# Two attention and two FFN layers on one core: a start with products on zeros, split weight loads, a shifted norm and a last tile in halves

## The chip, the core and the metric

The kernel runs on one core of a Trainium2 chip. Its engines run side by side and wait for one another through semaphores: TensorE (PE in the profile, with PEld for its weight loads), VectorE (DVE), ScalarE (ACT), GpSimd (POOL) and SyncE (SP), which issues all DMAs here. Every engine works through its own instructions in the order in which the program writes them. The metric is the device time of one execution in microseconds, the median of several.

## What is computed

Four layers on x of 2048 rows by 1024 columns: linear attention (A), a gated FFN (B), then A and B again with the same weights. Each normalises its input first and adds its result to x.

```python
def _A_ref(x, wqkv, wo):                      # H = 32 heads of 32
    q, k, v = heads(x @ wqkv)
    pq, pk = phi(q), phi(k)                   # t+1 where t > 0, exp(t) elsewhere, + 1e-6
    kv = einsum("bhsd,bhse->bhde", pk, v);  z = einsum("bhsd->bhd", pk)
    o = einsum("bhqd,bhde->bhqe", pq, kv) / (einsum("bhqd,bhd->bhq", pq, z)[..., None] + 1e-6)
    return merge(o) @ wo
def _B_ref(x, w_gate, w_up, w_down):          # 1024 -> 3584 -> 1024
    return ((x @ w_gate) * (x @ w_up)) @ w_down
for f in (A, B, A, B): x = x + f(layernorm(x))
```

## The kernel before

x stays on chip as 16 tiles `X[:, t, :]` of 128 rows. The order is written by hand (`manual_schedule`): what a function emits first runs first on its engine. Pools of buffers (`slots` of 128x4096 bf16, `temps` of 128x512 float32, `banks`, the 8 PSUM banks) are queues from which `get` takes the oldest.

**The start.** SP issues the loads in the order x0, x1, k0, x2, x3, k1, x4, v0, x5, x6, v1, x7 to x15 (lines 90 to 113): an x tile is 256 KB, k0, k1, v0, v1 are weight slabs of 1 MB (`load_cols`: 8 rows of 512 columns for each of 128 partitions). Then the preamble (the last loop of the kernel) runs, for the tiles t = 0 to 3, `ln_stats` (two `bn_stats` and a `bn_aggr` on DVE) and `ln_norm` (a Ln and an Exp on ACT, then the normalising `tensor_scalar` on DVE, L170); for tile 0 also `tr_tile`: eight transposes on PE (L187) into a PSUM bank and one copy on ACT (L188) into the transposed buffer xnT.

**Layer A, first stage** (`layer_A`, `kv_chunk`). 64 steps; step 0 is tile 0 with k0, step 1 tile 0 with k1, step 2 tile 1 with k0, step 3 tile 1 with k1, and so on: eight products (L369) each, then `phi` (an Exp on ACT, L193; two operations on DVE, L194 and L195) or, for v, a copy. The transposes of tiles 1, 2 and 3 are hung on steps 0, 1 and 3. So PE runs: step 0, transposes of tile 1, step 1, transposes of tile 2, steps 2 and 3, transposes of tile 3, step 4. ACT runs: Ln and Exp of tiles 0 to 3, the Exp of step 0, the copy of tile 1, the Exp of step 1, the copy of tile 2. All later tiles are transposed by DMA.

**Layer A, second stage.** Steps i = 0 to 43. A step emits `den_step(i-4)` (one product L501, Ln and Exp on ACT, a multiply on DVE, L509), `q_step(i)` (eight products L487 and `phi`) and `out_step(i-12)` (eight products L517, then the addition to X on DVE, L519). Eight L509 (c = 0 to 7) make the left operand of eight `out_step`s; the first of these is one step behind the last L509. In the first layer A steps 12 to 17 also carry maxima over the down weights on DVE (L222). `ahead_of` hangs the preparation of the FFN on these steps: for the tiles u = 0 to 7 `ln_stats` at 18+2u, `ln_norm` at 19+2u, the DMA transpose at 20+2u; loads of FFN weights (22, 28), their casts on ACT (25 to 28, 34 to 37), their sums on DVE (35, 41: L327), the sums of the transposed input (`t_sums`, 36 to 39: L349 to L357), and two loads and a POOL cast of down weights (36, 38, 40).

**Layer B.** `quad` (products L646) for the gate and up weights, then `down_seven` (products L868) for the down weights, in two passes over halves of the rows. In the last of seven stretches of the last pass (`final and i == 4`) the four tiles run one after the other: 14 products, an addition on DVE (L841) and a store of 128 KB (L768) for each.

Of the kernel before, what the change touches and what calls it, by code (L numbers as in the profile page):

```python
# [34 lines left out]
def kernel(  # L35
# [49 lines left out]
    def v3(s, n):  # L85
        return s[:].rearrange("p (k n) -> p k n", n=n)
# [4 lines left out]
    def load_x(t):  # L91
        nc.sync.dma_start(out=X[:, t, :], in_=x_view[:, t, :])

    def load_cols(view, n):
        s = slots.get()
        nc.sync.dma_start(out=v3(s, NB), in_=view[:, :, n * NB:(n + 1) * NB])
        return s

    nc.scalar.preload_act_table_set("natural_log_exp_and_others")
    wA = {}  # L100
    load_x(0)
    load_x(1)
    wA["k"] = [load_cols(wqkv_v, DC)]
    load_x(2)
    load_x(3)
    wA["k"].append(load_cols(wqkv_v, DC + 1))
    load_x(4)
    wA["v"] = [load_cols(wqkv_v, 2 * DC)]
    load_x(5)
# [2 lines left out]
    for t in range(7, NT):  # L112
        load_x(t)

    ident = const.tile([P, P], BF16, tag="ident", name="ident")
    make_identity(nc, ident[:])
    mask = const.tile([P, P], F32, tag="mask", name="mask")
# [33 lines left out]
    xqs = {}  # L151
    lns = {}

    def ln_stats(li, t):
        mv = small.tile([P, 2], F32, tag="mv", name="mv")
        st = small.tile([P, NST, 6], F32, tag="st", name="st")
        for c in range(NST):
            nc.vector.bn_stats(out=st[:, c, :], in_=X[:, t, c * FMAX:(c + 1) * FMAX])  # L158
        nc.vector.bn_aggr(out=mv[:], in_=st[:])
        lns[(li, t)] = mv  # L160

    def ln_norm(li, t):
        mv = lns[(li, t)]
# [10 lines left out]
    def tr_tile(li, t):  # L174
        xn = lns.pop((li, t))
        g, tl = divmod(t, TPG)
        if (li, g) not in xnTs:
            xnTs[(li, g)] = slots.get()
        s = xnTs[(li, g)]
        xnT = (h3 if li % 2 == 1 else v3)(s, NB)  # L180
        if (li, g) != (0, 0):
            nc.sync.dma_start_transpose(out=xnT[:, :, tl * P:(tl + 1) * P], in_=xn[:])
            return
        b = banks.get()
        pt = b[:].bitcast(BF16).rearrange("p (k n) -> p k n", n=P)
        for k in range(KD):
            nc.tensor.transpose(out=pt[:, k, :], in_=xn[:, k * P:(k + 1) * P], identity=ident[:])  # L187
        nc.scalar.copy(out=xnT[:, :, tl * P:(tl + 1) * P], in_=pt)  # L188
        banks.put(b)

    def phi(b, dst):
# [583 lines left out]
    def down_seven(q, li, p, hs, wd, load_piece, cast_piece, ORDER, at, run, finish, xrow, nl, W2, load_a, final):  # L775
        sg = [slots.get(), slots.get()]

        def blocks(r):
            v = hs[r][:].bitcast(F16).rearrange("p (u a g t) -> p u a g t", a=2, g=2, t=G)
            return [v[:, :, a, g, :] for g in range(2) for a in range(2)]  # L780

        def sview(r):
            return h3(sg[r // 4], G)[:, 2 * (r % 4):2 * (r % 4) + 2, :]

        def s_sum(i, r):
            a11, a12, a21, a22 = blocks(r)
            o = sview(r)
            x, y, op = {5: (a21, a22, ALU.add), 6: (o, a11, ALU.subtract), 3: (a12, o, ALU.subtract),
                        7: (a11, a21, ALU.subtract)}[i]
            nc.vector.tensor_tensor(out=o, in0=x, in1=y, op=op)  # L790

        def lhs(i, j, tl):
            if i in (1, 2, 4):
                v = blocks(j // 2)[{1: 0, 2: 1, 4: 3}[i]][:, j % 2, :]
            else:
                v = sview(j // 2)[:, j % 2, :]
            return v[:, tl * P:(tl + 1) * P]

        cast_piece(1)
        for i in range(2, 2 * len(ORDER)):  # L800
            at((i - 1) * WPC, cast_piece, i)
        for pi, i in enumerate(ORDER[:-1]):
            nx = ORDER[pi + 1]
            if nx in (5, 6, 3, 7):
                for r in range(NQD // 2):
                    at(pi * NQD + 2 * r + 1, s_sum, nx, r)
        if nl[0] < 4:
            for u in range(2 * TPG if p == 0 else TPG):
                t = nl[1] * 2 * TPG + u
                at(2 + 7 * u, ln_stats, nl[0], t)  # L810
                at(4 + 7 * u, ln_norm, nl[0], t)
                at(5 + 7 * u, tr_tile, nl[0], t)
        if not final:
            if p == 0:
                for i in range(4):
                    at(60 + 4 * i, t_sums, li, 1, i)
                if q == 0:
                    at(74, W2.load, 0)
                    at(77, W2.load, 1)
                    for i in range(4):  # L820
                        at(82 + i, W2.cast, 0, i)
                        at(86 + i, W2.cast, 1, i)
                    at(88, W2.sums, 0)
                    at(92, W2.sums, 1)
                    at(95, W2.store, 0)
                    at(97, W2.store, 1)
                else:
                    at(75, W2.load, 0)
                    at(89, W2.load, 1)
            else:  # L830
                at(16, load_a, "k", 0)
                at(30, load_a, "k", 1)
                at(44, load_a, "v", 0)
                at(75, load_a, "v", 1)

        bank = {}
        u = {}

        def read(o, g, tl, n, src, keep=None):
            _, x, _ = xrow(g, tl, n)  # L840
            nc.vector.scalar_tensor_tensor(out=o, in0=src, scalar=kap[:], in1=x if keep is None else keep,  # L841
                                           op0=ALU.mult, op1=ALU.add)

        def after(i, tl):
            b = bank[("a" if i in (1, 6, 7, 4) else "c" if i in (5, 3) else "b", tl)]
            if i in (1, 5, 6):
                g, n = {1: (0, 0), 5: (1, 1), 6: (0, 1)}[i]
                u[(i, tl)] = temps.get()
                read(u[(i, tl)][:], g, tl, n, b[:])
                return  # L850
            g, n, k = {3: (0, 1, 6), 7: (1, 1, 5), 2: (0, 0, 1), 4: (1, 0, None)}[i]
            t = u.pop((k, tl)) if k else None
            _, x, _ = xrow(g, tl, n)
            read(x, g, tl, n, b[:], t[:] if k else None)
            if k:
                temps.put(t)
            if i in (3, 2, 4):
                banks.put(b)
            finish(g, tl, n)

        for pi, i in enumerate(ORDER):
            if i in (1, 5, 2):
                for tl in range(TPG):
                    bank[({1: "a", 5: "c", 2: "b"}[i], tl)] = banks.get()
            key = "a" if i in (1, 6, 7, 4) else "c" if i in (5, 3) else "b"

            def mm(j, tl):
                nc.tensor.matmul(out=bank[(key, tl)][:], lhsT=lhs(i, j, tl),  # L868
                                 rhs=h3(wd[2 * pi + j // WPC], NB)[:, j % WPC, :],
                                 start=(j == 0 and i in (1, 5, 2)), stop=(j == NQD - 1), skip_group_check=True)  # L870

            if final and i == 4:
                for tl in range(TPG):
                    for j in range(NQD):
                        mm(j, tl)
                    after(i, tl)
                continue
            for j in range(NQD):
                for tl in range(TPG):
                    mm(j, tl)  # L880
                if j % WPC == WPC - 1:
                    slots.put(wd[2 * pi + j // WPC])
                    load_piece()
                if i == 7 and j == 7:
                    slots.put(sg[0])
                if i == 7 and j == NQD - 1:
                    slots.put(sg[1])
                if i == 4 and j % 2 == 1:
                    slots.put(hs[j // 2])
                run(pi * NQD + j)  # L890
            for tl in range(TPG):
                after(i, tl)

    def ahead_of(li, W):
        plan = {}

        def at(step, *what):
            plan.setdefault(step, []).append(what)

        for u in range(2 * TPG):  # L900
            at(18 + 2 * u, ln_stats, li, u)
            at(19 + 2 * u, ln_norm, li, u)
            at(20 + 2 * u, tr_tile, li, u)
        at(22, W.load, 0)
        at(28, W.load, 1)
        for i in range(4):
            at(25 + i, W.cast, 0, i)
            at(34 + i, W.cast, 1, i)
            at(36 + i, t_sums, li, 0, i)
        at(35, W.sums, 0)  # L910
        at(41, W.sums, 1)
        if li == 1:
            at(36, prep_load, 0)
            at(38, prep_load, 1)
            at(40, prep_cast, 0)
        return plan

    for t in range(TPG):
        ln_stats(0, t)
        ln_norm(0, t)  # L920
        if t == 0:
            tr_tile(0, 0)
    for li in (0, 2):
        W = Weights(li)
        layer_A(li, ahead_of(li + 1, W))
# [31 lines left out]
```

## Time and profile before

| what | value |
|---|---|
| median of 3 runs | 1515.68 us (1515.39 to 1516.0) |
| the profiled execution's own time | 1515.59 us |
| its span, first to last instruction | 1513.8 us |
| PE busy | 1499.7 us, 99% of the span |
| DVE, ACT, POOL busy | 63%, 49%, 6% |
| first product on weights / last one | starts at 9.62 us / starts at 1510.09 us |

Times are microseconds from the span's start. In the timeline a row gives start, length, engine, line, operation, output<-inputs, how many were merged, and in brackets the engine's idle time before it with what ended it. The rows themselves stand in the prediction.

### The profile page before, as it was taken

What the parts mean: (1) busy time and instruction counts of PE and PEld (TensorE: products, weight loads), DVE (VectorE), ACT (ScalarE), POOL (GpSimd) and SP (SyncE); (2) the same over time, 40 slices, a digit from 0 to 9 for tenths busy, and PEclk for the clock granted to TensorE, in tenths of its full rate; (3) what the DMA queues carried; (4) which work ended last, traced back from release to release, by engine and by line L of the source; (5) the groups of instructions that cost most, each with busy time, mean ns of one, the idle gap of its engine ahead of it and who ended that gap; (6) DMA issues with size and microseconds to landing.
All of it is one profiled execution on the core that took longest, in us unless ns stands there. A gap on an engine that the chain in (4) does not pass through costs nothing.

```text
span 1513.8 us, 18314 instructions
## 1 busy us (share of the span) xinstructions
PE 1499.7 (99%) x7155; PEld 689.1 (46%) x7155; DVE 952.5 (63%) x1595; ACT 736.2 (49%) x1111; POOL 90.0 (6%) x46
## 2 busy tenths in 40 slices
PE   7999999999999999999999999999999999999999
PEld 3454444444444444444445444444444444444444
DVE  6567998988677566667355467854444853444452
ACT  4677875777535477762133365523334222333420
POOL 0000004963000000000000000000000000000000
PEclk9999999999999999999999999999999999999999
DMA  7696246475358788758413300563333678333523
GB/s 239 152 302 225 84 90 189 121 218 159 117 135 240 239 264 263 243 197 247 160 28 84 84 1 8 148 234 139 140 111 129 165 258 342 113 139 139 193 75 129
DMA packets 213399, 247.61 MB, mean 164 GB/s; under 512 B 68416, under 2 KB 189248, under 8 KB 202560
## 3 DMA queue, kind: packets, MB, share of 16 engines
q1 hardware_dynamic: 213312, 246.44, 51.6%
q8 instruction: 56, 0.92, 0.2%
q14 instruction: 31, 0.25, 0.0%
HBM read 189.79 MB, written 40.89 MB: 152 GB/s over the span
## 4 chain that ended last, share of the span: by engine, by line
PE 94%; DVE 4%; ACT 1%; DMA 1%; issue 0%; SPq 0%
PE b L646 45%; PE b L868 22%; PE b L369 12%; PE b L517 6%; PE b L487 6%; PE b L386 1%; DVE dmx L222 1%; PE b L501 1%; ACT s L202 1%; DVE wst L207 1%; DVE f L195 1%; DMA s<-in_A_wqkv_dram 1%; DVE f L194 1%; ACT f L193 0%; DVE s L195 0%; PE b L469 0%
## 5 line engine op out<-in xcount | busy, mean ns | idle before, releaser
L646 PE MATMUL b<-s,s 128*128 128x512 f16 x3136 | 677.5, 379 | 0.0
L646 PEld LDWEIGHTS <-s 128*128 128x128 f16 x3136 | 306.9, 98 | 370.0
L868 PE MATMUL b<-s,s 128*128 128x512 f16 x1568 | 339.1, 379 | 0.0
L662 DVE TENSOR_TENSOR f<-f,b 128x512 f32<-128x512 f32 x232 | 159.0, 686 | 229.1 <-ACT f L651 214.6
L651 ACT COPY f<-b 128x512 f32<-128x512 f32 x284 | 165.9, 584 | 228.0 <-PE b L646 228.0
L868 PEld LDWEIGHTS <-s 128*128 128x128 f16 x1568 | 153.4, 98 | 185.0
L369 PE MATMUL b<-s,s 128*128 128x512 bf16 x1024 | 225.0, 381 | 2.5 <-DMA s<-in_A_wqkv_dram 2.2
L369 PEld LDWEIGHTS <-s 128*128 128x128 bf16 x1024 | 100.3, 98 | 122.7 <-issue 3.9
L193 ACT ACTIVATE f<-b 128x512 f32<-128x512 f32 x128 | 75.5, 595 | 106.5 <-PE b L369 85.7
L613 ACT ACTIVATE s<-s,scw 128x1792 f16<-128x1792 bf16 x48 | 83.1, 1785 | 90.7 <-DMA s<-in_B_w_down_dram 52.7
L312 ACT ACTIVATE s<-s,scw 128x1024 f16<-128x1024 bf16 x112 | 122.9, 1152 | 3.3 <-DMA s<-in_B_w_gate_dram 2.1
L657 ACT COPY b<-b 128x512 f32<-128x512 f32 x104 | 59.2, 570 | 128.3 <-PE b L646 128.3
L517 PE MATMUL b<-s,s 128*128 128x512 bf16 x512 | 118.5, 379 | 1.9 <-DVE s L509 1.9
L487 PE MATMUL b<-s,s 128*128 128x512 bf16 x512 | 120.3, 379 | 0.0
L571 POOL TENSOR_SCALAR s<-s,scw 128x1024 f16<-128x1024 bf16 x28 | 88.3, 3170 | 263.4 <-DVE X L519 246.1
L194 DVE TENSOR_SCALAR f<-f 128x512 f32<-128x512 f32 x128 | 53.9, 421 | 75.2 <-ACT f L193 74.3
L665 DVE SCALAR_TENSOR_TENSOR s<-f,b 128x512 f16<-128x512 f32 x108 | 74.1, 686 | 40.9 <-PE b L646 24.5
L665 DVE SCALAR_TENSOR_TENSOR s<-f,f 128x512 f16<-128x512 f32 x116 | 82.5, 711 | 4.0
L158 DVE BATCH_NORM_STATS2 st<-X 128x6 f32<-128x512 bf16 x128 | 81.8, 680 | 4.4 <-DMA X<-in_A_x_dram 4.4
L517 PEld LDWEIGHTS <-s 128*128 128x128 bf16 x512 | 50.1, 98 | 62.6 <-DVE s L509 2.4
L487 PEld LDWEIGHTS <-s 128*128 128x128 bf16 x512 | 50.0, 98 | 59.6
L841 DVE SCALAR_TENSOR_TENSOR X<-b,kap,f 128x512 bf16<-128x512 f32 x48 | 32.7, 744 | 60.6 <-PE b L868 60.6
(80 smaller groups left out, 850.6 us busy)
## 6 DMA issues: line engine op xcount, KB each, us to landing
s<-wc SPq DMA_DIRECT2D x56, 1024.0 KB, 6.2
s<-dc SPq DMA_DIRECT2D x32, 896.0 KB, 6.3
wc<-s SPq DMA_DIRECT2D x28, 1024.0 KB, 4.9
s<-in_B_w_down_dram SPq DMA_DIRECT2D x24, 896.0 KB, 5.1
s<-in_B_w_down_dram SPq DMA_DIRECT2D x14, 1024.0 KB, 7.4
s<-in_B_w_gate_dram SPq DMA_DIRECT2D x28, 512.0 KB, 5.8
s<-in_B_w_up_dram SPq DMA_DIRECT2D x28, 512.0 KB, 6.8
s<-in_A_wqkv_dram SPq DMA_DIRECT2D x12, 1024.0 KB, 8.9
```

The costliest lines, as they stand in the source:

```text
L158: nc.vector.bn_stats(out=st[:, c, :], in_=X[:, t, c * FMAX:(c + 1) * FMAX])
L312: nc.scalar.activation(out=h, in_=v, func=ACT.Copy, scale=scw[:, m:m + 1])
L369: nc.tensor.matmul(out=b[:], lhsT=xnT[:, k, tl * P:(tl + 1) * P], rhs=w[:, k, :], start=(k == 0), stop=(k == KD - 1))
L487: nc.tensor.matmul(out=b[:], lhsT=w[:, k, j * P:(j + 1) * P], rhs=xnT[:, k, :], start=(k == 0), stop=(k == KD - 1))
L517: nc.tensor.matmul(out=b[:], lhsT=v3(pqs[g], G)[:, c, tl * P:(tl + 1) * P], rhs=v3(M[n], NB)[:, c, :], start=(c == 0), stop=(c == KD - 1))
L571: nc.gpsimd.tensor_scalar(out=h3(s, D)[:, i, :], in0=v3(s, D)[:, i, :], scalar1=scw[:, 2:3], scalar2=None, op0=ALU.mult)
L613: nc.scalar.activation(out=v.bitcast(F16)[:, r * w:(r + 1) * w], in_=v[:, r * w:(r + 1) * w], func=ACT.Copy, scale=scw[:, 2:3])
L646: nc.tensor.matmul(out=o[m][:], lhsT=W.get(j, m, st[i - 1], k), rhs=mv[i - 1][:, k, :], start=start and k == 0, stop=stop and k == KH - 1, ...
L651: nc.scalar.copy(out=d[m][:], in_=o[m][:])
L662: nc.vector.tensor_tensor(out=d[m][:], in0=d[m][:], in1=o[m][:], op=ALU.add)
L665: nc.vector.scalar_tensor_tensor(out=hv[:, 2 * (j % 2) + r, g * G:(g + 1) * G], in0=x[:], scalar=HS, in1=y[:], op0=ALU.mult, op1=ALU.mult)
L868: nc.tensor.matmul(out=bank[(key, tl)][:], lhsT=lhs(i, j, tl), rhs=h3(wd[2 * pi + j // WPC], NB)[:, j % WPC, :], start=(j == 0 and i in (1 ...
```

## The change

Five edits. (1) A 128x512 float32 buffer is set to zero on DVE, and PE multiplies it by itself into a spare bank: 11 products ahead of everything, 4 more after the transposes of tile 0. Nothing reads the results. (2) k0 and k1 are loaded in two DMAs of 512 KB each, and k1 is issued ahead of x2 and x3. (3) One of the two `bn_stats` of tile 1 is emitted ahead of tile 0's normalisation, and the ACT copy after the PE transposes is split in two. (4) In `ahead_of` the norm and the transposes of the FFN's input are emitted 2 steps later, `t_sums` 3 steps later. (5) The last tile of the last stretch is computed, added and stored in two column halves of 256.

```diff
-    def load_cols(view, n):
+    def load_cols(view, n, parts=1):
         s = slots.get()
-        nc.sync.dma_start(out=v3(s, NB), in_=view[:, :, n * NB:(n + 1) * NB])
+        w = KD // parts
+        for r in range(parts):
+            nc.sync.dma_start(out=v3(s, NB)[:, r * w:(r + 1) * w, :],
+                              in_=view[:, r * w:(r + 1) * w, n * NB:(n + 1) * NB])
...
     load_x(1)
-    wA["k"] = [load_cols(wqkv_v, DC)]
+    wA["k"] = [load_cols(wqkv_v, DC, 2)]
+    wA["k"].append(load_cols(wqkv_v, DC + 1, 2))
     load_x(2)
     load_x(3)
-    wA["k"].append(load_cols(wqkv_v, DC + 1))
...
+    warm = temps.get()
+    nc.vector.memset(warm[:], 0.0)
+    warmb = banks.get()
+
+    def warm_up(n):
+        for _ in range(n):
+            nc.tensor.matmul(out=warmb[:], lhsT=warm[:].bitcast(BF16)[:, 0:P], rhs=warm[:].bitcast(BF16)[:, 0:NB],
+                             start=True, stop=True)
+
+    warm_up(11)
...
-        nc.scalar.copy(out=xnT[:, :, tl * P:(tl + 1) * P], in_=pt)
+        nc.scalar.copy(out=xnT[:, 0:KH, tl * P:(tl + 1) * P], in_=pt[:, 0:KH])
+        nc.scalar.copy(out=xnT[:, KH:KD, tl * P:(tl + 1) * P], in_=pt[:, KH:KD])
...
             if final and i == 4:
-                for tl in range(TPG):
+                for tl in range(TPG - 1):
...
+                t, x, d = xrow(1, TPG - 1, 0)
+                b = bank[(key, TPG - 1)]
+                for h in range(2):
+                    w = slice(h * NB // 2, (h + 1) * NB // 2)
+                    for j in range(NQD):
+                        nc.tensor.matmul(out=b[:, w], lhsT=lhs(i, j, TPG - 1),
+                                         rhs=h3(wd[2 * pi + j // WPC], NB)[:, j % WPC, w],
+                                         start=False, stop=(j == NQD - 1), skip_group_check=True)
+                    nc.vector.scalar_tensor_tensor(out=x[:, w], in0=b[:, w], scalar=kap[:], in1=x[:, w],
+                                                   op0=ALU.mult, op1=ALU.add)
+                    nc.sync.dma_start(out=d[:, w], in_=x[:, w])
...
-            at(18 + 2 * u, ln_stats, li, u)
-            at(19 + 2 * u, ln_norm, li, u)
-            at(20 + 2 * u, tr_tile, li, u)
+            at(20 + 2 * u, ln_stats, li, u)
+            at(21 + 2 * u, ln_norm, li, u)
+            at(22 + 2 * u, tr_tile, li, u)
...
-            at(36 + i, t_sums, li, 0, i)
+            at(39 + i, t_sums, li, 0, i)
...
-    for t in range(TPG):
+    ln_stats(0, 0)
+    ln_stats(0, 1, (0,))
+    ln_norm(0, 0)
+    tr_tile(0, 0)
+    ln_stats(0, 1, (1,))
+    ln_norm(0, 1)
+    for t in range(2, TPG):
         ln_stats(0, t)
         ln_norm(0, t)
-        if t == 0:
-            tr_tile(0, 0)
+    warm_up(4)
+    temps.put(warm)
+    banks.put(warmb)
```

`ln_stats` gets a list of the parts that it computes; the statistics buffer is kept between the two calls.

## The prediction

> **What bounds the kernel now.** I read the page's busy shares and chain first. PE is busy for 1499.7 of 1513.8 us, and the chain that ended last is 94% PE. So only three things can move the end: time in which PE stands, time in which its products run slowly, and the tail after the last product. The waits view names where PE stands:
>
> ```profile
> PE 94%; DVE 4%; ACT 1%; DMA 1%; issue 0%; SPq 0%
> ...
> PE b L187 <- DVE xn L170: 6.4, 1, 6.4
> PE b L369 <- DMA s<-in_A_wqkv_dram: 2.2, 1, 2.2
> PE b L517 <- DVE s L509: 1.9, 1, 1.9
> PE b L369 <- DVE s L195: 0.2, 1, 0.2
> ```
>
> The reader is to see four waits: 6.4 + 2.2 us ahead of the first products, 1.9 us once in the second stage, 0.2 us that no edit touches. Then the timeline of the start, for PE, ACT and DVE:
>
> ```profile
> 9.62 3.57 PE L369 MATMUL b<-s,s 128*128 128x512 bf16 x8 [2.22 <-DMA s<-in_A_wqkv_dram]
> 12.98 1.06 PE L187 MATMUL b<-ident,xn 128*128 128x128 bf16 x8
> 14.04 2.29 PE L369 MATMUL b<-s,s 128*128 128x512 bf16 x8
> 16.17 0.61 PE L187 MATMUL b<-ident,xn 128*128 128x128 bf16 x8
> 16.62 3.62 PE L369 MATMUL b<-s,s 128*128 128x512 bf16 x16
> ...
> 10.33 1.29 DVE L158 BATCH_NORM_STATS2 st<-X 128x6 f32<-128x512 bf16 x2 [0.88 <-DMA X<-in_A_x_dram]
> 12.92 1.28 DVE L158 BATCH_NORM_STATS2 st<-X 128x6 f32<-128x512 bf16 x2
> 14.23 0.21 DVE L159 BATCH_NORM_AGGREGATE mv<-st 128x2 f32<-128x12 f32 x1
> ...
> 14.48 0.29 ACT L166 ACTIVATE rstd<-mv,eps 128x1 f32<-128x1 f32 x1 [2.05 <-DVE mv L159]
> 14.80 0.20 ACT L168 ACTIVATE rstd<-rstd 128x1 f32<-128x1 f32 x1
> 14.91 0.58 ACT L193 ACTIVATE f<-b 128x512 f32<-128x512 f32 x1
> 15.39 1.00 ACT L188 COPY s<-b 128x1024 bf16<-128x1024 bf16 x1
> ```
>
> Step 0 takes 3.36 us from its start to the next PE row (0.42 a product), steps 2 and 3 take 3.45 us for sixteen (0.216): PE runs at half speed up to about 14.9 us, which the granted clock of the page (1.00 throughout) does not show. The ACT rows matter most. ACT stands 2.05 us for tile 3's statistics, and the copy of tile 1, which steps 2 and 3 need, is behind them in its queue. It ends at 16.39, just ahead of the products at 16.62. So two chains arrive together at 16.62: cold PE, and x2's landing -> statistics of tiles 2 and 3 -> Ln, Exp -> copy of tile 1. After 16.62 PE runs gapless but for the 0.2 and the 1.9 us.
>
> **The start, part by part.** The landings (issue plus the trace's time to landing) are x1 4.1, k0 9.6, x2 10.3, x3 11.0, k1 14.0, x4 14.7, v0 17.7: in order of issue, 0.7 us for an x tile, 3.0 for a slab, and 5.5 for the first slab. The change puts k1, 3.0 us of transfer, ahead of x2. With the same bytes ahead of it x2 lands at 10.3 + 3.0 = 13.3. If the split removes the first slab's excess (5.5 against 3.0), it is 4.1 + 3.0 + 3.0 + 0.7 = 10.8. I take 12.8, near the upper end, since the slab's own row is the nearest. Issuing costs nothing: two more DMAs at 0.4 us each (L92 and L96 rows), while the transfers queue for 8 to 10 us.
>
> From x2's landing to the products of step 2 the chain is now: 10.3 -> Ln of tile 3 at 14.48 (4.2 us) -> copy at 15.39 (0.9: Ln, Exp, the Exp of step 0) -> 1.0 copy. With halved copies (about 0.58 for 512 columns, the L193 row) the first four products need only the first half: 4.2 + 0.9 + 0.55 + 0.2 = 5.85 us. So step 2 starts at 12.8 + 5.85 = 18.65, against 16.62: **+2.0 us**, with ends 10.8 + 5.85 - 16.62 = 0.0 and 13.3 + 5.85 - 16.62 = +2.5. What the warm clock, the split k0 and the earlier k1 save ahead of step 2 is hidden by this chain: PE would have step 1 done about 1.3 us after k1's last half (k1 is one x tile ahead of x2, so 12.1 + 1.1 = 13.2), then stands to 15.5 for tile 2 (x2 + 2.7, as 10.3 -> 13.0 now), does eight transposes (0.45), and stands again to 18.65. Even without the move of k1 the copy of tile 1 would leave 0.2 to 0.6 us to gain.
>
> The zeros themselves cost nothing: the memset (some 0.4 us, the 128x512 L194 row) falls ahead of DVE's first work at 3.56, and 11 cold products at 0.43 are 4.7 us, done ahead of the transposes at 6.36 if they start by 1.6. The 4 later ones (0.9 to 1.7 us) stand in the wait for k0. If that cover were gone, they would cost their 1.7 us. The split `bn_stats` (0.68) goes into DVE's 0.66 us wait for rstd.
>
> **What the clock does in that new wait.** Between step 1 and step 2 lie about 5.5 us with 0.45 us of transposes. The only such gap that this trace shows is its end:
>
> ```profile
> 1510.50:1513.30 2.80, 0.00 (x0) 0.00 (x0) 0.75 (x1) 0.00 (x0) 0.00 (x0) 1.00 0.14 47
> 1513.30:1513.80 0.50, 0.00 (x0) 0.00 (x0) 0.00 (x0) 0.00 (x0) 0.00 (x0) 0.55 0.00 0
> ```
>
> PE's last product ends at 1510.47; the granted clock (third column from the right) is 1.00 up to 1513.30 and 0.55 over the last 0.5 us, so it halves 2.8 to 2.9 us after the last product. At the start it came back 5.3 us after products began (9.62 to 14.9). I expect the fall (4 in 5), then 3 to 5.3 us at half speed, which costs half of that, 1.5 to 2.65: I take **+2.1**, with ends 0 (no fall) and 3.4 (6.8 us).
> [...]
> [...]
>
> **The norm 2 steps later.** The wait of 1.9 us, on DVE:
>
> ```profile
> 191.55 1.28 DVE L158 BATCH_NORM_STATS2 st<-X 128x6 f32<-128x512 bf16 x2
> 192.86 0.21 DVE L159 BATCH_NORM_AGGREGATE mv<-st 128x2 f32<-128x12 f32 x1
> 192.99 0.37 DVE L509 TENSOR_TENSOR s<-f,f 128x512 bf16<-128x512 bf16 x1
> ...
> 193.42 0.39 PE L517 MATMUL b<-s,s 128*128 128x512 bf16 x1 [1.93 <-DVE s L509]
> ```
>
> DVE runs two steps behind PE here, and the statistics of u = 0 stand ahead of the eighth L509. Two steps later they stand behind it: L509 starts at 191.55, the product at 193.42 - 1.44 = 191.98. **-1.4 us**; the ends are 0 and -2.1 (the product could start at 189.82 + 7 x 0.216 = 191.33; 0.65 us stay). What is late next: u = 7's statistics move to step 34, its transpose to step 36, and `t_sums` to 39 to 42. DVE was solid from 242.8 to 258.2, then idle 4.3 us to 262.5; the four `t_sums` (1.2 to 1.5 us each) end near 259 instead of 253.2, and their last reader starts at 255.64 + 9 x 0.864 = 263.4. On SP the weight loads of steps 22 and 28 stand behind one transpose fewer, the loads of steps 36 and 38 behind u = 7's transpose, some 3 us later; POOL's cast (248.63, four of 3.17) then ends near 264, and its reader L629 is at 273.3. All covered. In the second layer A, DVE waits between additions at the stage's end (1.0 us each), so more so.
>
> **The last tile.** Now: last product starts at 1510.09, addition 1510.50 to 1511.25 (0.75), store issued at 1511.28, landed 1.7 later. A half addition costs between 0.28 (L448, 128 columns out of PSUM) and 0.75; on the line between, 0.43. The 28 half products cost the same 3.02 us plus at most some 0.1 (32 products of 129 columns take 1.89, so the weight loads don't bind). **-0.3**; ends -0.6 (a store 0.2 faster) and +0.5 if the second half's products had to wait for the first half's addition in the same bank.
>
> **The sum** against the profiled 1515.59 (span 1513.8 and 1.8 around it): +2.0 + 2.1 - 1.4 - 0.3 = +2.4, so **1518.0**. The median of the runs, 1515.68, is 0.1 above.
>
> **Rivals.** (a) The clock holds in the gap: 2.1 less, 1515.9. For it, the transposes in its middle; against it, 2.9 us sufficed at the end. (b) The split removes the first slab's excess: x2 at 10.8, start 0.0, -1.7 for the rest, 1513.9, or 1516.0 if the clock falls. Against it, packets and their order stay. (c) Slower by over 3.0: x2 at 13.3 (+2.5) and the clock not back within 4.6 us of step 2; the place is steps 2 to 4, the price up to 2.65 (5.3 us, as at 9.62), 1519.0, and up to 1519.8 at 6.8 us. It decides once the start and the clock together cost over 4.7. (d) The zeros pay in full, x2 lands as early as now because queued DMAs share the engines: start at 10.3 + 5.85 = 16.15, -0.5, the sum -2.2, 1513.4. Against it, the landings in order. More than 3.0 us faster would need ACT to copy tile 1 ahead of tile 3's Ln, which its written order excludes; I leave it 0.06, with what I overlook.
>
> **How the numbers follow.** Forecast 0.39, (a) 0.17, (b) 0.11, (c) 0.27, (d) and beyond 0.06. A measurement of this kernel tells about 0.2% (3.0 us) from no change. Forecast, (a) and (b) lie within that: 0.67; slower 0.27; faster 0.06. The range takes (a), most of (b) and most of (c): 1514.4 to 1519.7.
>
> **What would show it.** Right: DVE's first `bn_stats` of tile 2 near 12.8; L166 of tile 3 about 4.2 us later; PE's row at steps 2 and 3 starting near 18.6 with an idle time released by ACT L188, and products 0.43 us apart there; 0.5 to 0.7 us left at L517. Wrong: step 2 ahead of 16.6, or no idle time between steps 1 and 2.

## The result, and the profile after

| | before | after |
|---|---|---|
| median (17 executions of each, one chip) | 1515.55 us (1514.90 to 1516.46) | 1519.02 us (1517.99 to 1520.04) |
| profiled execution, and its span | 1515.59, 1513.8 us | 1518.39, 1516.6 us |

The ratio is 1.0023, with an interval of 1.0015 to 1.0030: 3.5 us slower. The profiled executions differ by 2.8 us only, since the one of after is among the quicker of its 17; the rows below explain 2.8 us.

The waits of PE after the change, with the total, the number and the longest of each:

```profile
PE b L202 <- DVE xn L185: 3.2, 2, 2.4
PE b L385 <- ACT s L203: 1.9, 1, 1.9
...
PE b L533 <- DVE s L525: 0.9, 2, 0.6
PE b L898 <- DVE X L901: 0.6, 1, 0.6
PE b L385 <- DMA s<-in_A_wqkv_dram: 0.5, 1, 0.5
```

In place of 6.4 and 2.2 us ahead of the first products stand 2.4 us for tile 2's normalised rows and 1.9 us for the copy of tile 1 (L203 is now the first half of it). The one wait of 1.9 us in the second stage has become two with a sum of 0.9 us, and the last tile (L898) has a wait that it did not have. The start in the timeline, PE first, then the statistics of tile 2 on DVE, which wait for x2, then ACT:

```profile
6.75 1.03 PE L124 MATMUL b<-f 128*128 128x512 bf16 x4
7.61 2.10 PE L385 MATMUL b<-s,s 128*128 128x512 bf16 x8
9.54 0.61 PE L202 MATMUL b<-ident,xn 128*128 128x128 bf16 x8
10.18 1.02 PE L385 MATMUL b<-s,s 128*128 128x512 bf16 x4
11.66 1.02 PE L385 MATMUL b<-s,s 128*128 128x512 bf16 x4 [0.45 <-DMA s<-in_A_wqkv_dram]
15.03 1.04 PE L202 MATMUL b<-ident,xn 128*128 128x128 bf16 x8 [2.35 <-DVE xn L185]
17.99 5.32 PE L385 MATMUL b<-s,s 128*128 128x512 bf16 x16 [1.92 <-ACT s L203]
...
12.30 1.28 DVE L172 BATCH_NORM_STATS2 st<-X 128x6 f32<-128x512 bf16 x2 [3.27 <-DMA X<-in_A_x_dram]
...
16.45 0.29 ACT L181 ACTIVATE rstd<-mv,eps 128x1 f32<-128x1 f32 x1 [2.05 <-DVE mv L175]
16.77 0.20 ACT L183 ACTIVATE rstd<-rstd 128x1 f32<-128x1 f32 x1
16.88 0.58 ACT L209 ACTIVATE f<-b 128x512 f32<-128x512 f32 x1
17.36 0.58 ACT L203 COPY s<-b 128x512 bf16<-128x512 bf16 x1
```

Step 1 starts 3.9 us earlier than before (10.18, was 14.04), and all of it is lost again: step 2 starts at 17.99, was 16.62. ACT shows why. Tile 3's Ln (L181) still waits 2.05 us, and the copy of tile 1 is still behind it, only that x2, on which both statistics rest, now lands at 12.28 and not at 10.30. And the sixteen products of steps 2 and 3 take 5.32 us, where they took 3.62. The stretches between the records of the granted clock (mean clock in the third column from the right):

```profile
11.49:14.62 3.13, 1.02 (x4) 0.29 (x3) 1.69 (x4) 0.50 (x2) 0.00 (x0) 1.00 1.08 359
14.62:21.45 6.83, 4.50 (x17) 2.03 (x18) 4.48 (x9) 3.41 (x8) 0.00 (x0) 0.50 1.08 365
```

The first record at full clock starts at 4.38, among the zeros, whose weight loads stand 0.43 us apart up to 4.40 and about 0.22 from there; the clock fell at 14.62 in the gap and was back at 21.45, 3.46 us after step 2 had started. From there on the two traces differ by a constant, and it changes at three places only:

| PE reaches | before | after | difference |
|---|---|---|---|
| step 2 | 16.62 | 17.99 | +1.37 |
| step 4 | 20.52 | 23.59 | +3.07 |
| eighth product of `out_step` 20 | 193.42 | 195.11 | +1.69 |
| layer B | 255.64 | 257.87 | +2.23 |
| last tile | 1507.28 | 1509.50 | +2.22 |
| end | 1513.81 | 1516.61 | +2.80 |

The step from 1.69 to 2.23 lies at `out_step` 36, where DVE has the statistics of the last tile, u = 7, ahead of a multiply (L525, the former L509):

```profile
243.69 1.28 DVE L172 BATCH_NORM_STATS2 st<-X 128x6 f32<-128x512 bf16 x2
245.00 0.21 DVE L175 BATCH_NORM_AGGREGATE mv<-st 128x2 f32<-128x12 f32 x1
245.13 0.37 DVE L525 TENSOR_TENSOR s<-f,f 128x512 bf16<-128x512 bf16 x1
...
245.56 6.65 PE L533 MATMUL b<-s,s 128*128 128x512 bf16 x30 [0.36 <-DVE s L525]
```

It is the wait of before in small: before, u = 0's statistics stood ahead of the eighth L509; now u = 7's stand ahead of the one of step 35. (By the starts of the products 0.54 us are lost, of which the view calls 0.36 idle.) And the end, first the last addition of before, then the rows of after:

```profile
1510.50 0.75 DVE L841 SCALAR_TENSOR_TENSOR X<-b,kap,X 128x512 bf16<-128x512 f32 x1 [2.27 <-PE b L868]
...
1509.50 1.69 PE L898 MATMUL b<-s,s 128*128 128x256 f16 x14
...
1511.23 0.48 DVE L901 SCALAR_TENSOR_TENSOR X<-b,kap,X 128x256 bf16<-128x256 f32 x1 [0.78 <-PE b L898]
...
1511.77 1.69 PE L898 MATMUL b<-s,s 128*128 128x256 f16 x14 [0.58 <-DVE X L901]
...
1513.49 0.48 DVE L901 SCALAR_TENSOR_TENSOR X<-b,kap,X 128x256 bf16<-128x256 f32 x1 [1.78 <-PE b L898]
```

The second half's products start (1511.77) when DVE has read the first half out of the same bank (1511.23 + 0.48 = 1511.71). The last addition is 0.27 us shorter (0.48 for 0.75), the wait costs 0.75, and from its end to the end of the span it takes 2.64 us, not less than the 2.56 before. (Over all thirteen traces this is 2.63 to 2.65 us with halves and 2.54 to 2.73 with the whole tile.)

### The profile page after: what moved, and what is told of

It reads as the page before. It is cut to its first block, busy times and chain, and to the rows that moved or that the text cites. A ratio compares the mean times of both kernels' runs of the same rounds, so it can differ in the third digit from the quotient of the medians.

```text
span 1516.6 us, 18379 instructions
## 1 busy us (share of the span) xinstructions
PE 1504.6 (99%) x7184; PEld 691.4 (46%) x7184; DVE 954.1 (63%) x1597; ACT 737.0 (49%) x1115; POOL 89.0 (6%) x46
## 4 chain that ended last, share of the span: by engine, by line
PE 92%; DVE 5%; ACT 1%; DMA 1%; issue 0%; SPq 0%; DVEq 0%
PE b L662 45%; PE b L884 22%; PE b L385 12%; PE b L503 6%; PE b L533 6%; PE b L402 1%; DVE dmx L238 1%; ACT s L218 1%; PE b L517 1%; DVE wst L223 1%; DVE f L211 1%; DVE f L210 1%; DVE st L172 1%; DMA X<-in_A_x_dram 1%; DVE X L535 0%; ACT f L209 0%
```

## The experiments

Theory: the order of the loads and ACT's queue set step 2, the gap that this opens lets the clock fall, the norm and the tail each carry a small new wait. Times are medians of 11 executions, and each ratio is against the kernel before on the same chip. Experiments 1 to 4, 5 to 8 and 9 to 11 ran on one chip each, so across these groups the ratios are the fairer comparison.

**1. x2 and x3 ahead of k1 again** (order_back)

```diff
-    wA["k"].append(load_cols(wqkv_v, DC + 1, 2))
     load_x(2)
     load_x(3)
+    wA["k"].append(load_cols(wqkv_v, DC + 1, 2))
```

> The changed kernel with x2 and x3 issued ahead of k1 again (both slabs still in halves). Theory (x2's landing sets step 2 through ScalarE's queue, and the wait that it makes lets the clock fall): x2 lands near 9.3 (8.6 for k0's second half plus 0.7), step 2 starts 5.7 later, near 15.0 instead of 17.99, and the clock holds or falls for a short time only; step 4 starts near 18.9 instead of 23.59; the time is about 4.7 us below the changed kernel, 1514.3, under the kernel before. Rival (the split loads or the products on zeros cost the time, not the order): x2 earlier, but step 4 stays within 1 us of 23.6 and the time within 1 us of 1519.0.

1513.93 us, ratio 0.9993 (0.9984 to 1.0002); x2 lands at 9.26. PE's rows:

```profile
13.00 1.02 PE L385 MATMUL b<-s,s 128*128 128x512 bf16 x4 [0.47 <-DMA s<-in_A_wqkv_dram]
13.86 0.61 PE L202 MATMUL b<-ident,xn 128*128 128x128 bf16 x8
15.20 3.40 PE L385 MATMUL b<-s,s 128*128 128x512 bf16 x15 [0.73 <-ACT s L203]
...
18.88 6.42 PE L385 MATMUL b<-s,s 128*128 128x512 bf16 x28
```

Step 1 is later by 1.3 us, step 2 earlier by 2.8, its fifteen products take 3.40 us, where sixteen took 5.32 in after. So the move of k1 costs 4.5 us (by the ratios; 5.1 by the medians), and without it the change is no slower than before. The rival, that the zeros or the split loads cost the time, is out. In 4 of the 11 executions the mean granted clock is 0.999 and the median time 1515.14, in the other 7 it is 1.000 and 1513.71.

**2. Zeros in the gap** (fill_gap)

```diff
-    def warm_up(n):
+    def warm_up(n, b=warmb):
...
         b = banks.get()
+        if t == 2:
+            warm_up(11, b)
         pt = b[:].bitcast(BF16).rearrange("p (k n) -> p k n", n=P)
...
             b = banks.get()
+            if (li, t, n) == (0, 1, 0):
+                warm_up(10, b)
```

> The changed kernel with 11 more products on zeros ahead of the transposes of tile 2 and 10 more ahead of step 2, where PE stood for 2.35 and 1.92 us. Theory (the gap lets the clock fall; step 2's start is set by the copies on ScalarE): step 2 still starts at 18.0, its products stand 0.216 apart instead of 0.427, no fall of the granted clock ahead of the end, and the time is 1.7 us less in the profile (half of 3.46 us at half speed), about 2 us in the median. Rival (zeros don't count as work for the clock, or the fall has nothing to do with the gap): products at 0.427 again, time unchanged within 0.5 us.

1516.71 us, ratio 1.0010 (1.0001 to 1.0019), with clock 1.000 in all 11 executions.

```profile
12.69 2.54 PE L124 MATMUL b<-f 128*128 128x512 bf16 x10
15.20 0.62 PE L204 MATMUL b<-ident,xn 128*128 128x128 bf16 x8
15.66 2.32 PE L124 MATMUL b<-f 128*128 128x512 bf16 x10
18.16 3.63 PE L389 MATMUL b<-s,s 128*128 128x512 bf16 x16 [0.18 <-ACT s L205]
...
22.07 8.15 PE L389 MATMUL b<-s,s 128*128 128x512 bf16 x36
```

Step 2 starts as late as in after, but its products take 3.63 us. Step 4 comes at 22.07 and not 23.59: the price of the fall by itself is 1.5 us in the traces (1.7 from step 2 on) and 2.0 by the two ratios.

**3. ACT's order mended** (queue_fix): Ln and Exp of tiles 2 and 3 behind the copy of tile 1, k1 as in after.

```diff
-    for t in range(2, TPG):
-        ln_stats(0, t)
-        ln_norm(0, t)
     warm_up(4)
...
-            for t, i in ((1, 0), (2, 1), (3, 3)):
-                at(i, tr_tile, li, t)
+            at(0, tr_tile, li, 1)
+            at(0, ln_stats, li, 2)
+            at(0, ln_norm, li, 2)
+            at(0, ln_stats, li, 3)
+            at(2, tr_tile, li, 2)
+            at(2, ln_norm, li, 3)
+            at(4, tr_tile, li, 3)
```

> The changed kernel with its load order, but with ScalarE's Ln and Exp of tiles 2 and 3 emitted behind the copy of tile 1 (statistics of tiles 2 and 3 and norm of tile 2 at step 0, norm of tile 3 at step 2, transposes of tile 2 at step 2, of tile 3 at step 4). Theory (the copy of tile 1 stands in ScalarE's queue behind tile 3's Ln): step 2 follows step 1 directly near 12.5, the transposes of tile 2 wait for x2 up to 15.0, step 4 starts near 17.2 and step 6 near 21.4 instead of 27.05; the clock holds; the time falls by about 5.6 us, to 1513.4, under the kernel before. Rival (x2's landing itself holds PE, whatever the order on ScalarE): step 4 not before 20, gain under 3 us.

1512.90 us, ratio 0.9986 (0.9978 to 0.9995), clock 1.000 in all executions. ACT, then PE:

```profile
10.59 0.58 ACT L203 COPY s<-b 128x512 bf16<-128x512 bf16 x1
11.05 0.61 ACT L204 COPY s<-b 128x512 bf16<-128x512 bf16 x1
14.24 0.29 ACT L181 ACTIVATE rstd<-mv,eps 128x1 f32<-128x1 f32 x1 [2.58 <-DVE mv L175]
...
12.02 2.75 PE L385 MATMUL b<-s,s 128*128 128x512 bf16 x11 [0.46 <-DMA s<-in_A_wqkv_dram]
15.41 0.62 PE L202 MATMUL b<-ident,xn 128*128 128x128 bf16 x8 [0.65 <-DVE xn L185]
```

The copy is done at 11.66, ahead of the Ln, and step 2 follows step 1 without a gap (the row of eleven products runs across both). With the copy free, the early k1 pays: 5.6 us below after by the ratios, 6.1 by the medians, and 1.0 below experiment 1 on the same chip, where the two intervals overlap. The order of the loads was not bad in itself; it was bad with that queue.

**4. The norm alone, on the kernel before** (norm_only)

```diff
-            at(18 + 2 * u, ln_stats, li, u)
+            at(20 + 2 * u, ln_stats, li, u)
...
-            at(36 + i, t_sums, li, 0, i)
+            at(39 + i, t_sums, li, 0, i)
```

> The kernel before with the norm of the FFN 2 steps later and nothing else. Theory (1.4 us saved at the eighth product of out_step 20, 0.5 us given back at out_step 36, where tile 7's statistics now stand ahead of the last L509): two waits at that line, 0.6 and 0.4 us of idle time, and the time 0.85 us below the kernel before. Rival (the second wait comes from the later start of the changed kernel): one wait, 1.4 us less.

1514.36 us against 1515.25, ratio 0.9993 (0.9984 to 1.0002): 0.9 us less, as expected, but the interval takes in no change at all. What carries the reading is the trace, with the two waits of after: 0.55 us at step 20 and 0.35 at step 36. So the second wait does not come from the later start of the changed kernel.

**5. The zeros alone, on the kernel before** (zeros_only): the buffer, the bank and the 11 + 4 products.

> The kernel before with the products on zeros alone (11 and 4), its load order, whole slabs and whole copies kept. Theory (x2's landing sets step 2 through ScalarE, so the warm clock is hidden): the clock is up ahead of step 0, PE waits for k1 and then for the copy of tile 1, step 2 starts 6.1 us after x2's landing, and the time is 0.2 to 0.5 us less, up to 1.0 where x2 lands early. Rival (the cold products of the start were the bound): step 2 comes 2 us or more earlier relative to x2's landing and the time is 2 us less or better.

1516.22 us, ratio 1.0006 (0.9997 to 1.0015): no gain, and the expectation missed. Its eleven executions fall into two groups. Five with a mean clock of 1.000 take 1514.68 to 1515.79, median 1515.10, 0.4 below the kernel before, as expected; six with 0.999 or 0.998 take 1516.22 to 1517.92, median 1517.06. (In after 6.83 us at half speed go with a mean of 0.998.) PE in the profiled one, whose clock held:

```profile
8.66 1.89 PE L379 MATMUL b<-s,s 128*128 128x512 bf16 x8 [0.78 <-DMA s<-in_A_wqkv_dram]
10.39 0.61 PE L197 MATMUL b<-ident,xn 128*128 128x128 bf16 x8
13.05 1.89 PE L379 MATMUL b<-s,s 128*128 128x512 bf16 x8 [2.05 <-DMA s<-in_A_wqkv_dram]
...
15.68 3.40 PE L379 MATMUL b<-s,s 128*128 128x512 bf16 x15 [0.30 <-ACT s L198]
```

A PE that is warm early only waits for k1 (2.05 us); in after the clock fell in such a wait (2.35 us, at 14.62). That it falls there in the slower group was not profiled; it is inferred from the clock of those executions. This kernel also keeps the 1.9 us wait at `out_step` 20, and which of the two waits it was is not shown; the profiled execution has both waits and a mean clock of 1.000.

**6. Experiment 3 with the last tile whole** (tail_whole)

```diff
-                for tl in range(TPG - 1):
+                for tl in range(TPG):
                     for j in range(NQD):
                         mm(j, tl)
                     after(i, tl)
...
```

The loop over the two halves is taken out.

> The kernel queue_fix with the last tile whole again, as in the kernel before. Theory (the second half's products wait 0.75 us for the first half's addition in the same bank, the shorter addition gives 0.27 back): no wait at the last tile, last product to end of span 3.7 us as in the kernel before, the time 0.6 us less than queue_fix, 1512.3. Rival (the longer tail is the two stores or the half products): the gain is under 0.2 us.

1512.38 us, ratio 0.9979 (0.9970 to 0.9988), no wait in the tail; 0.5 us below experiment 3 by the medians and 1.1 by the ratios, with overlapping intervals. The traces show the size: from the start of the last tile to the end it is 6.69 us here and 7.11 in after, 6.52 to 6.71 in all nine traces with a whole tile and 7.11 to 7.13 in all four with halves.

**7. The same with the norm shifted by 1 step and not 2** (norm_odd): `ln_stats` at 19 + 2u, `ln_norm` at 20 + 2u, the transpose at 21 + 2u, `t_sums` at 38 + i.

> The kernel tail_whole with the norm of the FFN 1 step later than in the kernel before instead of 2 (statistics at odd steps 19 to 33, t_sums at 38 to 41). Theory (statistics that stand directly ahead of the last L509 of a group hold PE): the wait of 0.35 to 0.5 us at out_step 36 is gone, the one at out_step 20 stays at about 0.6 since VectorE is late there by itself; the time is 0.5 us less than tail_whole, 1511.8. Rival (the second wait comes from VectorE's total load near the end of the stage): both waits stay.

1513.93 us, ratio 0.9990 (0.9982 to 0.9999): 1.5 us slower where 0.5 faster was expected. PE waits 1.94 us at `out_step` 36, and the releaser has moved to ACT:

```profile
240.56 12.48 PE L538 MATMUL b<-s,s 128*128 128x512 bf16 x56 [1.94 <-DVE s L530]
...
237.24 0.29 ACT L181 ACTIVATE rstd<-mv,eps5x 128x1 f32<-128x1 f32 x1 [2.42 <-DVE mv L175]
...
237.67 1.13 ACT L328 ACTIVATE s<-s,scw 128x1024 f16<-128x1024 bf16 x1
238.71 0.67 ACT L524 ACTIVATE f<-b,eps 128x512 f32<-128x512 f32 x1
239.41 0.63 ACT L527 ACTIVATE f<-f 128x512 bf16<-128x512 f32 x1
...
240.07 0.42 DVE L530 TENSOR_TENSOR s<-f,f 128x512 bf16<-128x512 bf16 x1 [1.53 <-ACT f L527]
```

u = 7's Ln waits 2.42 us for its statistics at the head of ACT's queue; behind it stand a weight cast (1.13 us) and the Ln and Exp of step 35, for which DVE and so PE wait.

**8. Experiment 7 without the zeros** (no_zeros)

```diff
-    warm_up(11)
...
-    warm_up(4)
```

> The kernel norm_odd without the products on zeros (the memset stays). Theory (once ScalarE's queue no longer holds step 2, PE itself is the bound of the start, and the clock is worth what the products lose): step 0 at half speed, clock up 3.4 to 6.8 us after it; step 6 some 2 us later; the time 2 us (1.5 to 3) more than norm_odd, 1513.8. Rival (waits for loads still cover the cold products): under 0.7 us more.

1514.83 us, ratio 0.9997 (0.9988 to 1.0006): 0.9 more than with them on the same chip, between the two expectations, with overlapping intervals. Step 0 takes 3.29 us for its eight products, where it takes 1.89 with the zeros; from 11.22 on, 3.1 us after step 0's start and not 3.4 to 6.8, eight transposes take 0.61 us, where the first eight took 1.04. The products behind the transposes of tile 2 start at 16.30 in place of 14.70, so not all of the 1.6 us shows in the medians.

**9. Experiment 6 with u = 7 one step later still** (late7)

```diff
-            at(20 + 2 * u, ln_stats, li, u)
-            at(21 + 2 * u, ln_norm, li, u)
-            at(22 + 2 * u, tr_tile, li, u)
+            s = 20 + 2 * u + (u == 7)
+            at(s, ln_stats, li, u)
+            at(s + 1, ln_norm, li, u)
+            at(s + 2, tr_tile, li, u)
```

> The kernel with the repaired order of the start and the whole last tile, with the statistics, norm and transpose of u = 7 one step later still (steps 35, 36 and 37 in place of 34, 35 and 36). Theory: the 0.35 to 0.55 us wait at out_step 36 of the first layer A comes from u = 7's statistics, which stand ahead of the DVE multiply of step 35; one step later they stand behind it, the wait is gone, the one at out_step 20 stays, and the time is 0.4 to 0.5 us below that kernel: about 1511.9 us, span 1510.6. Rival: the wait moves on by one step, since u = 7's transpose at step 37 now stands ahead of the last products or ScalarE's queue is in the way as with the odd steps: no gain, or 1 us and more lost.

1511.87 us, ratio 0.9976 (0.9967 to 0.9985), the best of all, though the 0.5 us below experiment 6 lie within the intervals. The trace shows more: PE's waits for L530 are one of 0.6 us, at step 20; DVE now has the multiply first:

```profile
238.57 0.43 DVE L530 TENSOR_TENSOR s<-f,f 128x512 bf16<-128x512 bf16 x1 [0.37 <-ACT f L527]
...
239.51 1.28 DVE L172 BATCH_NORM_STATS2 st<-X 128x6 f32<-128x512 bf16 x2
```

**10. Experiment 6 with whole slabs** (whole_slabs): `load_cols` with one part for k0 and k1.

> The kernel with the repaired order of the start and the whole last tile, with the first two weight slabs loaded whole and not in halves. Theory: the halves are worth nothing by themselves, since the zeros keep the clock up or bring it up and statistics set step 2: within 0.3 us of that kernel, about 1512.4 us (ratio to the kernel before 0.998). Rival: the halves let step 0 start 1.4 us earlier, and with them the clock does not fall in the wait for the first slab, as it did in executions of the kernel with the zeros alone: without them 1 to 2 us longer, with a wider spread.

1512.53 us, ratio 0.9980 (0.9972 to 0.9989): the halves are worth nothing that can be measured in the median. One of the 11 executions has clock 0.999, and it is the longest with 1514.86. With halves and the same start there was none in experiments 3, 6 and 9, but 2 of 11 in experiment 7, and the kernel before, in this group of runs, has 3 of 27. One in eleven is too few to say more.

**11. The changed kernel with its last tile whole** (after_whole_tail): the edit of experiment 6.

> The changed kernel with its last tile done whole again, as before the change. Theory: the column halves cost the 0.6 us by which the tail grew, since PE stands 0.75 us for the first half's addition in the same bank: about 1518.4 us, 0.6 below the changed kernel, with 3.3 to 3.9 us from the last product to the end and no wait ahead of it. Rival: the halves pay for their wait by the smaller last store, and the whole tile is no faster (within 0.2 us of 1519.0).

1518.54 us, ratio 1.0021 (1.0012 to 1.0030): 0.48 below after by the medians and 0.3 by the ratios, with overlapping intervals, so the time alone does not rule out the rival. The trace shows the size better: no wait in the last tile, and 6.70 us from its start to the end in place of 7.11.

## Why the prediction was right, and where its terms were off

The time of 1519.02 lies in the range of 1514.4 to 1519.7, and the two causes that the forecast named for it, a late step 2 and a fall of the clock, are what made the kernel slower. But it is 1.0 us above the 1518.0, and with +0.23% it lies just beyond the 0.2% within which the prediction had put 0.67 of its chances: its total is that of rival (c), slower by over 3.0, though not by (c)'s mechanism: the start and the clock together cost 3.1 us, and (c) needed over 4.7.

| term | predicted | in the traces |
|---|---|---|
| step 2 starts | +2.0 | +1.37 |
| the clock falls in the gap | +2.1 | +1.70 |
| the norm | -1.4 | -1.38 at step 20, +0.54 at step 36 |
| the last tile | -0.3 | +0.58 |
| sum | +2.4 | +2.8 |

- **The start.** Right in mechanism. "DVE's first `bn_stats` of tile 2 near 12.8" came at 12.30; from x2's landing to step 2 it took 5.71 us (5.85 predicted), and tile 2's transposes came at 15.03 (x2 + 2.75; + 2.7 predicted). Of the 0.6 us too much 0.5 are x2's landing, 12.28 and not 12.8. Step 1 ended 0.9 us after k1's second half had landed (11.61); the prediction gives 1.3 in words and 1.1 in its sum, and no term rests on either. The reason given for the choice, whether the split shortens the first slab, is not what decides: k0 is complete at 8.30, 8.62, 8.66 and 9.57 in the four traces with whole slabs, and at 7.81 to 9.26 in those with halves. These overlap, so rival (b) is not shown, and one trace was too few to price the first slab from. The halves after the first land 1.5 us apart (8.64, 10.14 and 11.61 in after), where a whole slab took 3.0, so two more DMAs cost nothing that shows.
- **The clock.** The fall came, so rival (a) was wrong; experiment 2, in which it did not come, puts its price at 1.5 to 2.0 us. The clock was low for 6.83 us, the upper end of the prediction; no row of before shows that figure, nor the 3 us at the lower end, and of its low times only the 5.3 us (9.62 to 14.9) come from rows. Products ran in 3.46 of the 6.83 us only, and half of that is the 1.7. The reason given, that it halves 2.8 to 2.9 us after the last product, does not hold: here it fell at 14.62, 2.1 us after step 1's last product (11.66 + 4 x 0.216 = 12.5; 1.9 by the end of the row, 12.68), and at the end of the span 2.9 us after the last row of products in before (1513.35) and 3.0 in after (1516.48). PE was at work for 1.02 of the 3.13 us ahead of the fall; what sets its moment is not shown. The transposes in the middle of the gap, on which rival (a) counts, tell nothing of it, since they began at 15.03, after the fall. In 14 executions of after the mean clock is 0.998, in 3 it is 0.999, with medians of 1519.39 and 1518.22; what decides between the two is not shown.
- **The norm.** The gain at step 20 is as worked out (0.55 us left, 0.5 to 0.7 predicted). What failed is the step "all covered". It followed `t_sums`, the loads and POOL's cast to their readers, but not u = 7's own statistics, which move to step 34 and there meet DVE and PE at the same distance as u = 0's did before. 0.54 of 1.38 us are given back; the waits in the traces of experiments 4 and 9 show it from both sides.
- **The last tile.** The bound "+0.5 if the second half's products had to wait for the first half's addition in the same bank" is what happened, and it should have been the value. The store's share of the gain did not come either: 128 KB took 2.56 us from addition to end, 64 KB 2.64. How much the halves cost is known to 0.4 to 0.6 us: after with the whole tile (experiment 11) takes 6.70 us for it, before 6.53.
- **The zeros** cost nothing here, as said: hidden behind the loads. That what the warm clock saves "is hidden by this chain" held for after; with the chain removed (experiments 7 and 8) they are worth 0.9 us, and by themselves (experiment 5) nothing.

The errors of +1.0 us (start and clock) and of -1.4 (norm and tail) partly offset each other, and that is luck. Of the 1.0 us between 1518.0 and 1519.02 the terms explain 0.4; the other 0.6 is the distance of the profiled execution from the median of its kernel.

## What to carry to other kernels

Before a load is moved ahead of another, follow the later one to every engine's queue: here the same order of loads cost some 4.5 us with the written queue of ScalarE, and paid once the copy that step 2 needs stood ahead of the Ln that waits for x2. When a block of work is shifted to clear one wait, check both of its ends: the last piece can meet at the new place what the first piece met at the old. And splitting the last tile did not pay with both halves in one bank and an addition in between (7.11 us from its start to the end, 6.53 whole); halves in two banks were not tried.

## What the runs showed of the hardware

- The granted clock fell at 14.62 in after, in a wait of 2.35 us of PE, with PE at work for 1.02 of the 3.13 us before; it was back at 21.45, with PE at work for 4.50 of the 6.83 us between. In before one record at full clock runs from 14.90 to 1513.35, through the wait of 1.93 us ahead of 193.42. The records that end within the spans last 10.24, 6.83 and 1495.04 us in after and 1498.45 in before: 3, 2, 438 and 439 times 3.413 us.
- Products on zeros brought the clock up ahead of the products on weights. In after the zeros go from 0.43 to about 0.22 us apart at 4.40, 3.0 us after the first; in before the first record at full clock starts at 14.90, 5.3 us after the first product on weights. The eight products of step 0 take 1.89 us in order_back, fill_gap, zeros_only, norm_odd and whole_slabs, 3.57 in before and 3.29 in no_zeros. The eight transposes behind the eleven zeros take 0.62 us in after, order_back, zeros_only, norm_odd, late7 and whole_slabs, 0.79 in tail_whole and 1.00 in fill_gap and queue_fix; without zeros they take 1.04 (before, no_zeros). With zeros in the gap as well (fill_gap) the mean clock is 1.000 in all 11 executions, where it is 0.998 or 0.999 in the 17 of after.
- Executions with a mean clock below 1.000, beside the waits of PE in the profiled one: zeros_only 6 of 11 (2.05 us for a slab, 1.9 at `out_step` 20) and order_back 4 of 11 (1.34 us for a slab), with medians 2.0 and 1.4 us above those of their other executions; norm_odd and no_zeros 2 of 11 each (1.94 us at `out_step` 36); the kernel before 3 of 93 in the three groups of runs (1.9 us at `out_step` 20); queue_fix, tail_whole and late7, which have no wait of over 0.7 us behind the first products on weights, 0 of 33. But whole_slabs, which has none either, has 1 of 11, and where in those executions the clock fell was not profiled.
